# Attention and squared-ReLU kernel: every engine's instructions in written order, q and k transposed into PSUM banks of their own, and the first loads spread over three queues

## The chip, the cores and the metric

The kernel runs on one core of a Trainium2 chip. The metric is the device time of one execution in microseconds (us). The time before is the median of three runs.

## The reference

Two parts follow each other. The first is causal attention for 8 batch rows ("rows" from here on), 8 heads, 576 positions and a head size of 64. Heads 0 to 3 see the last 32 positions (sliding), heads 4 to 7 every fourth of the last 128 (dilated). The second is a feed-forward layer on the 4608 tokens that come out of it: `relu(x @ w_in)`, squared, times `w_out`. Everything comes and goes as float32.

```python
rel = pos[:, None] - pos[None, :]
mask_plain = (rel >= 0) & (rel < 32)
mask_dil = (rel >= 0) & (rel < 128) & (rel % 4 == 0)
attn = softmax(where(mask, q @ k.T / 8, -1e9))        # per row and head, 576 x 576
x = (attn @ v) as (4608 tokens, 512)
g = maximum(x @ w_in, 0) ** 2                         # w_in 512 x 2048
out = g @ w_out                                       # w_out 2048 x 512
```

## The kernel before

Work is cut in two ways. Attention goes by row `b` (576 tokens). The feed-forward layer goes by chunk `c` of 512 tokens, so there are 9 chunks; chunk `c` needs the attention of rows up to `c`. A chunk is 64 matmuls of 128 x 512 into `ph` tiles (`w_in`, called mm1 here; after every 4 a `ph` is done, ScalarE writes `rt` = relu, VectorE writes `g` = `rt`*`rt`) and 64 into `po` tiles (`w_out`, mm2; after every 16 ScalarE copies `po` to `ot` and SyncE's queue stores it).

Attention of a row has stages:

- Loads. `load_sliding_qk` puts q and k of the sliding heads in `sq`, `load_v` puts v in `sv` (sliding) and `sd` (dilated), all on SyncE's queue (SP). `load_dilated_qk` puts q and k of the dilated heads in `nd` on GpSimd's queue (POOL), which casts to float16 on the way. The two weights come on POOL's queue too.
- Casts. POOL turns `sq` into `nq`, `sv` into `vp` and `sd` into `vd`. Only row 0's `nq` is cast by ScalarE (q) and VectorE (k).
- Transposes. `t_sliding` (tile `pt`) and `t_dilated` (tile `pd`) transpose 12 blocks each on TensorE, k and q in the two banks of one tile; VectorE copies k and ScalarE copies q to `QKTp` and `QKTd`.
- Scores (`ps`, `pz`): ScalarE takes exp into `AT`, VectorE multiplies by the mask.
- Values (`pav`, `paw`): VectorE divides by the sums into `x`. TensorE transposes `x` (`px`, `py`) and VectorE copies it to `xT`, the input of mm1.

`attn(b)` is written between pieces of an earlier chunk: `moe_gen` is a generator that yields after every two matmuls, and `pump(n)` runs n such pieces. A chunk has 64 pieces. Row 1 is written beside the rest of chunk 0 and row `b` beside chunk `b-1`; chunks 7 and 8 come alone at the end.

What is written is not what runs: a scheduler takes the instructions and places them on each engine by its own estimate of when they are ready. It may move a load of row 1 ahead of a cast of row 0. Each engine then runs its list strictly in that order; on SP, an issue that waits holds back every issue behind it.

PSUM has two pools: `papool` with 2 tiles of two banks (all attention tiles) and `pmool` with 4 of one bank (`ph`, `po`). The pool `osb` has 3 `ot` tiles, so the copy of the fourth `po` of a chunk waits until the first `ot` is stored.

The parts that the change touches:

Of the kernel before, what the change touches and what calls it, by code (L numbers as in the profile page):

```python
# [17 lines left out]
def kernel(  # L18
# [32 lines left out]
    PADD = P - QD  # L51
    UW = 576
# [16 lines left out]
    QKTd = const.tile([P, 2, HH, 2, PADD + CL], FP16, name="QKTd")  # L69
# [11 lines left out]
    def load_sliding_qk(b):  # L81
        for i, src in enumerate((q, k)):
            nc.sync.dma_start(
                out=sq[:, i, :, :],
                in_=src[b, 0:HH].rearrange("h (p j) d -> p h (j d)", j=6),
            )

    def load_v(b):
        for m in range(NB):
            lo = QB * m - PADP  # L90
            p0 = PADP if m == 0 else 0
            nc.sync.dma_start(  # L92
                out=sv[p0:P, m, :, :],
                in_=v[b, 0:HH, lo + p0 : lo + P, :].transpose([1, 0, 2]),
            )
        vv = v[b, HH:H].rearrange("h (i c) d -> i h (c d)", c=DIL)
        nc.sync.dma_start(out=sd[PADD:P, 0, :, :], in_=vv[0:QD])
        nc.sync.dma_start(out=sd[:, 1, :, :], in_=vv[QD - PADD : CL])

    def load_dilated_qk(b):  # L100
        nd = natp.tile([QB, 2, 2, 12 * D], FP16, name=f"nd{b}", tag="nd")
        for i, src in enumerate((q, k)):
# [3 lines left out]
        return nd  # L106
# [24 lines left out]
    def cast_sliding_qk(b, engs):  # L131
        n = natp.tile([QB, 2, 6, HH, D], FP16, name=f"nq{b}", tag="nq")
        for i in range(2):
            for half in range(2):
                j0 = 3 * half
                copy(
                    engs[i],
# [5 lines left out]
    def cast_v_sliding():  # L143
# [3 lines left out]
    def cast_v_dilated():  # L147
# [17 lines left out]
    make_identity(nc, ident)  # L165
    reli = const.tile([P, QB], I16, name="reli")
    nc.gpsimd.iota(reli, pattern=[[1, QB]], base=0, channel_multiplier=-1)
# [17 lines left out]
    nc.vector.memset(QKTd[:, 1, :, :, 0:PADD], 0.0)  # L185
# [14 lines left out]
    def moe_gen(c):  # L200
        g = gp.tile([P, NFF, TOKC], FP16, name=f"g{c}", tag="g")
        for ffc in range(NFF):
            ph = pmool.tile([P, TOKC], FP32, name=f"ph{c}_{ffc}", tag="pm")
            for dmk in range(NDM):
# [3 lines left out]
                    xT[:, dmk, c * TOKC : (c + 1) * TOKC],  # L208
# [8 lines left out]
            yield  # L217
        for t in range(TOKC // P):
            po = pmool.tile([P, DM], FP32, name=f"po{c}_{t}", tag="pm")
            for ffc in range(NFF):  # L220
                nc.tensor.matmul(  # L221
                    po,
                    g[:, ffc, t * P : (t + 1) * P],
                    wo[:, ffc, :],
                    start=(ffc == 0),
                    stop=(ffc == NFF - 1),
                )
                if ffc % 2 == 1 and ffc < NFF - 1:
                    yield
            ot = osb.tile([P, DM], FP32, name=f"ot{c}_{t}", tag="ot")  # L230
            nc.scalar.copy(ot, po)  # L231
            nc.sync.dma_start(
                out=out[(c * 4 + t) * P : (c * 4 + t + 1) * P, :], in_=ot
            )
            yield

# [15 lines left out]
    def t_sliding(b, n, hp):  # L252
        pt = pa(f"pt{b}_{hp}", FP16)
        for i in (1, 0):
            for j in range(6):
                nc.tensor.transpose(  # L256
                    pt[:, i, QB * j : QB * (j + 1)],
                    n[:, i, j, 2 * hp : 2 * hp + 2, :],
                    ident[0:QB, 0:QB],
                )  # L260
        for i, eng in ((1, nc.vector), (0, nc.scalar)):
            copy(
                eng,
                QKTp[:, i, hp, PADP:].rearrange("x (p j) -> x p j", j=6),
                pt[:, i, 0:UW].rearrange("x (j p) -> x p j", j=6),
            )

    def t_dilated(b, n, g):
        pt = pa(f"pd{b}_{g}", FP16)
        for i in (1, 0):  # L270
            for j in range(6):
                nc.tensor.transpose(  # L272
                    pt[:, i, QB * j : QB * (j + 1)],
                    n[:, i, g, P * j : P * (j + 1)],
                    ident[0:QB, 0:QB],
                )
        for i, eng in ((1, nc.vector), (0, nc.scalar)):
            for h in range(2):
                copy(
                    eng,  # L280
                    QKTd[:, i, 2 * g + h, :, PADD:].rearrange("x a (p s) -> x a p s", s=3),
                    pt[:, i, 0:UW].rearrange("x (s a h p) -> x a h p s", a=2, h=2, p=48)[
                        :, :, h
                    ],
                )
# [22 lines left out]
    def s_dilated(b, g):  # L308
        tiles = [pa(f"pz{b}_{g}_{h}") for h in range(2)]
        for h, ps in enumerate(tiles):  # L310
            for a in range(2):
                for t in range(2):
                    for e in range(2):
# [4 lines left out]
                            QKTd[r, 1, 2 * g + h, a, QD * t : QD * t + P],  # L318
                            QKTd[r, 0, 2 * g + h, a, PADD + QD * t : PADD + QD * (t + 1)],
# [48 lines left out]
    def x_sliding(b, half, xs):  # L368
        px = pa(f"px{b}_{half}", FP16)
        for m3 in range(3):  # L370
            m = 3 * half + m3
            x = xs[m // 2][:, m % 2].rearrange("p h d -> p (h d)")
            for c in range(2):
                nc.tensor.transpose(
                    px[:, 0, 288 * c + QB * m3 : 288 * c + QB * (m3 + 1)],
# [4 lines left out]
        nc.vector.tensor_copy(  # L380
            xT[:, 0:2, t0 : t0 + 288],
            px[:, 0, 0:UW].rearrange("x (c t) -> x c t", c=2),
        )

    def x_dilated(b, t, xs):
        py = pa(f"py{b}_{t}", FP16)
# [117 lines left out]
```

## Time and profile before

| What | Value |
|---|---|
| Time, median of 3 runs | 355.31 us (355.0 to 355.32) |
| The profiled execution | 355.09 us, of which 353.3 us are the span of its instructions |
| TensorE matmul busy | 318.3 us (90%) |
| VectorE, ScalarE, GpSimd busy | 192.2 us (54%), 158.9 us (45%), 83.2 us (24%) |
| DMA | 40.81 MB by the bytes that the packets wrote, mean 116 GB/s |
| Chain that ended last | PE 61%, DMA 16%, ACT 7%, DVE 6% |

In the rows of the profile PE is TensorE, PEld its weight loads, DVE VectorE, ACT ScalarE, POOL GpSimd; SPq and POOLq are the queues' issues. `[6.85 <-DMA nd]` behind an instruction says that its engine had been idle for 6.85 us and what ended that. A matmul's busy time overlaps that of its neighbours, so the distance between two starts is the better measure of what a matmul costs.

### The profile page before, as it was taken

The numbers are of one execution on the slowest core, as the hardware profiler recorded it, in microseconds if no ns is written. First come the engines' busy times: TensorE is split into PE (matmuls) and PEld (weight loads), VectorE is DVE, ScalarE is ACT, GpSimd is POOL, SyncE is SP. The second block draws the span as 40 slices with busy tenths as digits, with TensorE's granted clock in tenths as the row PEclk, the third lists the DMA queues.
The fourth block names the chain that finished last, engine by engine and source line by source line (L and its number), as shares of the span: only waits on it lengthen the run. The fifth ranks groups of instructions, "written<-read, shape, count | busy, mean of one in ns | idle before, by whom it ended". The sixth has DMA issues, their size and how long they took to land.

```text
span 353.3 us, 6704 instructions
## 1 busy us (share of the span) xinstructions
PE 318.3 (90%) x2656; PEld 164.3 (46%) x2656; DVE 192.2 (54%) x422; ACT 158.9 (45%) x296; POOL 83.2 (24%) x130
## 2 busy tenths in 40 slices
PE   0468875996999999999999999999999999999995
PEld 0355332553455545554555455545554554444442
DVE  2676951764874576557655775577557653402400
ACT  3250641605931594149414941494149415614611
POOL 3471527057252322232223222002200000000000
PEclk9999996999999999999999999999999999999999
DMA  8999999959994482448243424300110011011011
GB/s 183 224 211 202 208 254 194 207 131 258 248 196 129 141 170 58 129 128 188 58 125 118 67 58 129 115 2 3 61 60 0 2 68 52 0 61 59 1 61 60
DMA packets 49840, 40.81 MB, mean 116 GB/s; under 512 B 26000, under 2 KB 44688, under 8 KB 49808
## 3 DMA queue, kind: packets, MB, share of 16 engines
q1 hardware_dynamic: 42528, 31.46, 35.1%
q0 software_dynamic: 7280, 8.92, 15.0%
q8 instruction: 21, 0.34, 0.4%
q14 instruction: 11, 0.09, 0.1%
HBM read 39.85 MB, written 9.44 MB: 139 GB/s over the span
## 4 chain that ended last, share of the span: by engine, by line
PE 61%; DMA 16%; ACT 7%; DVE 6%; issue 4%; POOL 2%; SPq 2%; POOLq 0%; ACTq 0%
PE po L221 31%; PE ph L205 22%; DMA sq<-in_k_dram 5%; DMA wi<-in_moe_w_in_dram 4%; DMA sq<-in_q_dram 3%; ACT rt L215 3%; DVE QKTd L129 3%; DVE g L216 2%; DMA sv<-in_v_dram 2%; SPq L92 2%; PE paw L359 2%; DMA out_dram<-ot 2%; ACT QKTd L127 1%; PE pt L256 1%; POOL nq L129 1%
## 5 line engine op out<-in xcount | busy, mean ns | idle before, releaser
L205 PE MATMUL ph<-xT,wi 128*128 128x512 f16 x576 | 139.1, 382 | 2.3 <-ACT rt L215 1.0
L221 PE MATMUL po<-wo,g 128*128 128x512 f16 x576 | 140.1, 381 | 0.0
L215 ACT ACTIVATE rt<-ph 128x512 f16<-128x512 f32 x144 | 84.9, 608 | 36.2 <-PE ph L205 32.8
L216 DVE TENSOR_TENSOR g<-rt 128x512 f16<-128x512 f16 x144 | 68.7, 480 | 58.5 <-ACT rt L215 56.0
L205 PEld LDWEIGHTS <-wi 128*128 128x128 f16 x576 | 51.6, 98 | 57.5 <-issue 3.7
L231 ACT COPY ot<-po 128x512 f32<-128x512 f32 x36 | 21.1, 586 | 121.4 <-PE po L221 110.7
L221 PEld LDWEIGHTS <-g 128*128 128x128 f16 x576 | 51.4, 98 | 50.2 <-issue 0.6
L129 POOL CAST nq<-sq 96x768 f16<-96x768 f32 x28 | 24.1, 894 | 43.3 <-PE pt L256 20.7
L145 POOL CAST vp<-sv 128x512 f16<-128x512 f32 x24 | 16.3, 682 | 74.3 <-PE pav L345 35.3
L150 POOL CAST vd<-sd 128x512 f16<-128x512 f32 x32 | 19.5, 624 | 32.9 <-PE paw L359 25.6
L288 ACT ACTIVATE AT<-ps 128x576 f16<-128x576 f32 x32 | 19.8, 671 | 11.2 <-PE ps L298 11.2
L331 DVE TENSOR_TENSOR x_d<-paw,rcp_d 72x512 f16<-72x512 f32 x32 | 22.0, 686 | 1.1
L272 PE MATMUL pd<-ident,nd 96*128 96x96 f16 x192 | 12.1, 219 | 10.2 <-DMA nd<-in_k_dram 6.8
L256 PE MATMUL pt<-ident,nq 96*128 96x96 f16 x192 | 11.7, 215 | 10.1 <-DVE nq L129 9.6
L129 DVE COPY QKTp<-pt 128x576 f16<-128x576 f16 x16 | 12.0, 756 | 14.1 <-PE pt L256 14.1
L288 ACT ACTIVATE AT<-pz 128x576 f16<-128x576 f32 x32 | 19.1, 650 | 0.1
L289 DVE TENSOR_TENSOR AT<-AT,maskp 128x576 f16<-128x576 f16 x32 | 15.0, 468 | 7.5 <-ACT AT L288 5.1
L129 DVE COPY QKTd<-pd 128x288 f16<-128x288 f16 x32 | 13.0, 448 | 9.2 <-PE pd L272 9.1
L272 PEld LDWEIGHTS <-nd 96*128 96x128 f16 x192 | 11.1, 105 | 14.0 <-issue 10.9
L398 DVE COPY xT<-py 128x576 f16<-128x576 f16 x16 | 12.1, 757 | 9.9 <-PE py L392 9.9
L256 PEld LDWEIGHTS <-nq 96*128 96x128 f16 x192 | 10.6, 103 | 13.6 <-DVE nq L129 9.6
L289 DVE TENSOR_TENSOR AT<-AT,maskd 128x576 f16<-128x576 f16 x32 | 15.1, 474 | 3.2 <-ACT AT L288 0.3
(51 smaller groups left out, 194.5 us busy)
## 6 DMA issues: line engine op xcount, KB each, us to landing
out_dram<-ot SPq DMA_DIRECT2D x36, 256.0 KB, 2.4
sv<-in_v_dram SPq DMA_DIRECT2D x40, 128.0 KB, 4.4
sq<-in_q_dram SPq DMA_DIRECT2D x8, 576.0 KB, 10.5
sq<-in_k_dram SPq DMA_DIRECT2D x8, 576.0 KB
sd<-in_v_dram SPq DMA_DIRECT2D x8, 512.0 KB
nd<-in_q_dram POOLq DMA_DIRECT2D x16, 144.0 KB, 5.8
nd<-in_k_dram POOLq DMA_DIRECT2D x16, 144.0 KB, 6.0
sd<-in_v_dram SPq DMA_DIRECT2D x8, 288.0 KB
```

The costliest lines, as they stand in the source:

```text
L129: eng.tensor_copy(o, i)
L150: nc.gpsimd.tensor_copy(vd[:, t, c : c + 2, :, 0:D], sd[:, t, :, D * c : D * (c + 2)].rearrange("p h (c d) -> p c h d", d=D),)
L205: nc.tensor.matmul(ph, wi[:, dmk, ffc * P : ffc * P + P], xT[:, dmk, c * TOKC : (c + 1) * TOKC], start=(dmk == 0), stop=(dmk == NDM - 1),)
L215: nc.scalar.activation(rt, ph[:], ACTF.Relu)
L216: nc.vector.tensor_mul(g[:, ffc, :], rt, rt)
L221: nc.tensor.matmul(po, g[:, ffc, t * P : (t + 1) * P], wo[:, ffc, :], start=(ffc == 0), stop=(ffc == NFF - 1),)
L231: nc.scalar.copy(ot, po)
L256: nc.tensor.transpose(pt[:, i, QB * j : QB * (j + 1)], n[:, i, j, 2 * hp : 2 * hp + 2, :], ident[0:QB, 0:QB],)
L272: nc.tensor.transpose(pt[:, i, QB * j : QB * (j + 1)], n[:, i, g, P * j : P * (j + 1)], ident[0:QB, 0:QB],)
L288: nc.scalar.activation(AT[:, u, 0:UW], ps[:, :, 0 : UW // 2], ACTF.Exp, scale=scale)
L289: nc.vector.tensor_mul(AT[:, u, 0:UW], AT[:, u, 0:UW], mask)
L331: nc.vector.tensor_tensor(out=x[0:w], in0=pv[:, :, :, 0:D], in1=rcp[0:w].unsqueeze(3).to_broadcast([w, 2, HH, D]), op=ALU.mult,)
```

## The change

The scheduler is switched off (`manual_schedule`): each engine gets its instructions in the order of the program text, and the text is rearranged. With it come these edits.

1. Row 0's loads. k of the sliding heads and both dilated v loads are issued from ScalarE's queue; q and sliding v stay on SP. POOL makes `reli` and the identity first, and loads dilated k before q. The cast of k is shared by VectorE and POOL, that of q stays on ScalarE.
2. q and k are transposed into a bank each (`pt`, `pd` are now one-bank tiles, four times two per row), from `pmool`, or from `papool` in row 1, where `po` holds all four banks of `pmool`. `QKTd` has another layout. `px` and `py` come from `pmool` too, and ScalarE instead of VectorE copies them to `xT`.
3. Row 0 alternates transposes and scores. Row 1's loads come after three `ph` of chunk 0; row 1's q and k go before `w_out`, its v after its sliding transposes.
4. Chunk 0's mm2 runs over four `po` at once, four rows of `w_out` at a time (`mm2_by_rows_gen`), so that it can start when a quarter of `w_out` is there. All four outputs are then done at the end.
5. From row 2 on: transposes with 2 pieces of mm1 after each half, scores with 4 after each, values with 2 (1 in row 2).

```diff
+    ctx.enter_context(tc.manual_schedule())
...
-    load_sliding_qk(0)
-    nds = {0: load_dilated_qk(0)}
-    load_v(0)
+    load_sliding_qk(0, (nc.sync, nc.scalar))
+    reli = const.tile([P, QB], I16, name="reli")
+    nc.gpsimd.iota(reli, pattern=[[1, QB]], base=0, channel_multiplier=-1)
+    make_identity(nc, ident)
+    nds = {0: dilated_buffer(0)}
+    load_dilated_qk(0, nds[0])
+    load_sliding_v(0)
+    load_dilated_v(0, nc.scalar)
...
+    def mm2_by_rows_gen(c, g):
+        pos = [
+            pmool.tile([P, DM], FP32, name=f"po{c}_{t}", tag="pm") for t in range(TOKC // P)
+        ]
+        for f4 in range(0, NFF, 4):
+            for t, po in enumerate(pos):
+                for ffc in range(f4, f4 + 4):
+                    mm2(c, g, po, t, ffc)
+                    if ffc % 2 == 1 and ffc < NFF - 1:
+                        yield
+                if f4 + 4 == NFF:
+                    store(c, t, po)
+                    yield
...
+    def pt(name, wide):
+        if wide:
+            return pa(name, FP16)[:, 0, :]
+        return pmool.tile([P, 1024], FP16, name=name, tag="pm")
+
+    def t_sliding(b, n, hp, i, wide=False):
+        p_ = pt(f"pt{b}_{hp}_{i}", wide)
+        for j in range(6):
+            nc.tensor.transpose(
+                p_[:, QB * j : QB * (j + 1)],
+                n[:, i, j, 2 * hp : 2 * hp + 2, :],
+                ident[0:QB, 0:QB],
+            )
+        copy(
+            nc.vector if i else nc.scalar,
+            QKTp[:, i, hp, PADP:].rearrange("x (p j) -> x p j", j=6),
+            p_[:, 0:UW].rearrange("x (j p) -> x p j", j=6),
+        )
...
-    def attn(b, nq, nd, gap):
...
+    nq = cast_sliding_qk(0, (nc.scalar, nc.scalar, nc.vector, nc.gpsimd))
+    cast_sliding_v()
+    load_w_in()
+    cast_dilated_v()
+    for hp in range(2):
+        for i in (1, 0):
+            t_sliding(0, nq, hp, i)
+        s_sliding(0, hp)
...
+    g0 = hidden(0)
+    pending.append(mm1_gen(0, g0))
+    pump(6)
+    nds[1] = dilated_buffer(1)
+    nc.vector.memset(sq[:, :, :, 0:1], 0.0)
+    nc.vector.memset(nds[1][:, :, :, 0:1], 0.0)
+    load_sliding_qk(1)
+    load_dilated_qk(1, nds[1])
+    load_w_out()
+    nq = cast_sliding_qk(1, (nc.gpsimd,) * 4)
+    pump(26)
+    pending.append(mm2_by_rows_gen(0, g0))
+    for hp in range(2):
+        for i in (1, 0):
+            t_sliding(1, nq, hp, i, True)
+            pump(1)
+    nc.vector.memset(sv[:, 1, :, 0:1], 0.0)
+    nc.vector.memset(sd[:, 1, :, 0:1], 0.0)
+    load_v(1)
+    cast_v()
+    load_sliding_qk(2)
+    load_v(2)
+    nds[2] = dilated_buffer(2)
+    load_dilated_qk(2, nds[2])
...
+    attn_scores(1, 3)
+    attn_values(1, 1, True)
+    pump(1000)
...
+        transposes(b, nq, nds[b], 2)
+        attn_scores(b, 4)
+        attn_values(b, 1 if b == 2 else 2)
+        pump(1000)
```

What the order of the instructions shows at three places. First SP's queue before, from row 2's v (`sv`, `sd`) to the first stores of chunk 0 (`ot_0`, `ot_1`); the two `sq` rows after `sd` are row 3's, the third is row 4's q:

```order
L92 DMA sv<-in_v_dram 96x4x64
L92 DMA sv<-in_v_dram 128x4x64 x5
L97 DMA sd<-in_v_dram 72x4x256
L98 DMA sd<-in_v_dram 128x4x256
L83 DMA sq<-in_q_dram 96x4x384
L83 DMA sq<-in_k_dram 96x4x384
L83 DMA sq<-in_q_dram 96x4x384
L232 DMA out_dram<-ot_0_720 128x512
L92 DMA sv<-in_v_dram 96x4x64
L232 DMA out_dram<-ot_1_810 128x512
```

The same place on SP after the change, from row 2's `sq` on:

```order
L90 DMA sq<-in_q_dram 96x4x384
L90 DMA sq<-in_k_dram 96x4x384
L99 DMA sv<-in_v_dram 96x4x64
L99 DMA sv<-in_v_dram 128x4x64 x5
L106 DMA sd<-in_v_dram 72x4x256
L107 DMA sd<-in_v_dram 128x4x256
L251 DMA out_dram<-ot_0_882 128x512
L251 DMA out_dram<-ot_1_915 128x512
L251 DMA out_dram<-ot_2_945 128x512
L251 DMA out_dram<-ot_3_962 128x512
```

Row 3's q and k no longer stand ahead of the first store; all of row 2's loads still do, and all four stores now stand together.

Second ScalarE's list before, where chunk 0 ends and chunk 1 begins (`pz` are row 1's last scores, `pt` row 2's transposes):

```order
L288 ACTIVATE AT<-pz_1_1_755 128x576
L231 COPY ot_1_810<-po_1_723 128x512
L231 COPY ot_2_921<-po_2_821 128x512
L231 COPY ot_3_951<-po_3_934 128x512
L215 ACTIVATE rt_0_1002<-ph_0_955 128x512
L127 COPY QKTp<-pt_0_985 128x576
L215 ACTIVATE rt_1_1010<-ph_1_1005 128x512
L127 COPY QKTp<-pt_1_1013 128x576
```

The same place after the change:

```order
L431 COPY xT<-px_1_872 128x2x288
L250 COPY ot_0_882<-po_0_586 128x512
L250 COPY ot_1_915<-po_1_587 128x512
L449 COPY xT<-py_0_933 128x2x288
L250 COPY ot_2_945<-po_2_588 128x512
L449 COPY xT<-py_1_948 128x2x288
L250 COPY ot_3_962<-po_3_589 128x512
L235 ACTIVATE rt_0_971<-ph_0_966 128x512
L235 ACTIVATE rt_1_979<-ph_1_974 128x512
L235 ACTIVATE rt_2_987<-ph_2_982 128x512
L235 ACTIVATE rt_3_995<-ph_3_990 128x512
L235 ACTIVATE rt_4_1003<-ph_4_998 128x512
```

The copy to `ot_3`, which reuses `ot_0`'s tile, stands ahead of every `rt` of chunk 1 in both; the four `ot` copies have moved together to the end of row 1, and row 2's transposes have moved behind six `ph`.

Third POOL's list before, from row 0's v casts to row 1's q and k:

```order
L145 CAST vp<-sv 128x8x64 x3
L110 DMA wi<-in_moe_w_in_dram 128x4x512 x2
L110 DMA wi<-in_moe_w_in_dram 128x4x1024
L150 CAST vd<-sd 128x8x64 x4
L117 DMA wo<-in_moe_w_out_dram 128x4x512 x4
L105 DMA nd_502<-in_q_dram 48x2x768 x2
L105 DMA nd_502<-in_k_dram 48x2x768 x2
L129 CAST nq_579<-sq 96x768 x4
```

And after the change:

```order
L143 CAST nq_141<-sq 96x768
L159 CAST vp<-sv 128x8x64 x3
L124 DMA wi<-in_moe_w_in_dram 128x4x512 x2
L124 DMA wi<-in_moe_w_in_dram 128x4x1024
L164 CAST vd<-sd 128x8x64 x4
L120 DMA nd_456<-in_k_dram 48x2x768 x2
L120 DMA nd_456<-in_q_dram 48x2x768 x2
L131 DMA wo<-in_moe_w_out_dram 128x4x512 x4
L143 CAST nq_469<-sq 96x768 x4
```

`w_in` still stands right behind the casts of row 0's sliding v; row 1's dilated q and k have moved ahead of `w_out`.

More of the change, by code (lines that the diff above doesn't have):

```diff
@@ L51 @@
     PADD = P - QD
+    KPAD = 64
     UW = 576
@@ L217, in moe_gen, with mm2, store, mm2_gen @@
             yield
+    def mm2(c, g, po, t, ffc):
+        nc.tensor.matmul(
+            po,
+            g[:, ffc, t * P : (t + 1) * P],
+            wo[:, ffc, :],
+            start=(ffc == 0),
+            stop=(ffc == NFF - 1),
+        )
+    def store(c, t, po):
+        ot = osb.tile([P, DM], FP32, name=f"ot{c}_{t}", tag="ot")
+        nc.scalar.copy(ot, po)
+        nc.sync.dma_start(out=out[(c * 4 + t) * P : (c * 4 + t + 1) * P, :], in_=ot)
+    def mm2_gen(c, g):
         for t in range(TOKC // P):
@@ L220, in moe_gen, with hidden @@
             for ffc in range(NFF):
[L221 to L227, printed above, removed]
+                mm2(c, g, po, t, ffc)
                 if ffc % 2 == 1 and ffc < NFF - 1:
                     yield
[L230 to L234, printed above, removed]
-            yield
+            store(c, t, po)
+            yield
+    def mm2_by_rows_gen(c, g):
[5 more added lines that the diff above has]
+                for ffc in range(f4, f4 + 4):
+                    mm2(c, g, po, t, ffc)
+                    if ffc % 2 == 1 and ffc < NFF - 1:
+                        yield
+                if f4 + 4 == NFF:
+                    store(c, t, po)
+                    yield
+    def hidden(c):
+        return gp.tile([P, NFF, TOKC], FP16, name=f"g{c}", tag="g")
+    def moe_gen(c):
+        g = hidden(c)
+        yield from mm1_gen(c, g)
+        yield from mm2_gen(c, g)
     pending: list = []
@@ L423, in attn @@
             pump(gap)
[L424 to L431 removed]
+        x_sliding(b, 0, xs, wide)
+        pump(gap)
+        ys = [av_dilated(b, 0, 0)]
+        pump(gap)
+        x_sliding(b, 1, xs, wide)
+        pump(gap)
+        ys.append(av_dilated(b, 0, 1))
         pump(gap)
```

197 lines of the change are left out of this document (88 added, 109 removed).

## The prediction

> **What bounds the kernel now.** I read the slices of the page first, then the windows of the trace by row of attention, then the chain that ended last, then the engines' timelines around its waits.
>
> ```profile
> span 353.3 us, 6704 instructions
> PE   0468875996999999999999999999999999999995
> PEclk9999996999999999999999999999999999999999
> DMA  8999999959994482448243424300110011011011
> ```
>
> A slice is 8.83 us. TensorE is full from about the tenth slice on; before that it is not, and there DMA is. The kernel has a front of some 80 us that DMA paces and a steady part of 270 us that TensorE paces. The windows (PE, PEld, DVE, ACT, POOL busy, clock, DMA share, GB/s) put numbers to both:
>
> ```profile
> 0.00:70.00 70.00, 44.60 (x423) 25.37 (x423) 39.93 (x89) 27.43 (x50) 28.39 (x48) 0.95 1.12 210
> 55.00:60.00 5.00, 2.69 (x22) 1.47 (x23) 0.82 (x2) 0.33 (x1) 4.87 (x8) 0.50 1.17 172
> 116.34:151.99 35.65, 34.96 (x317) 18.30 (x316) 22.18 (x48) 17.79 (x34) 10.18 (x15) 1.00 0.52 127
> ...
> 187.64:223.30 35.66, 34.97 (x317) 18.30 (x316) 22.19 (x48) 17.79 (x34) 10.19 (x15) 1.00 0.38 93
> 223.30:258.50 35.20, 34.99 (x318) 18.31 (x317) 21.66 (x48) 17.79 (x34) 4.46 (x7) 1.00 0.09 35
> 258.50:293.70 35.20, 34.99 (x318) 18.31 (x317) 21.57 (x48) 17.79 (x34) 0.00 (x0) 1.00 0.08 31
> 293.70:321.30 27.60, 27.60 (x130) 12.48 (x129) 6.80 (x16) 11.90 (x20) 0.00 (x0) 1.00 0.10 39
> ```
>
> In 70 us the rings never empty: 210 GB/s. Rows 3, 4 and 5 take 35.65 us each, rows 6 and 7 35.20. The last line is a chunk without attention: 128 matmuls in 27.60 us, 0.2156 us each. So a row's attention costs TensorE 35.20 - 27.60 = 7.6 us where POOL is idle.
>
> Where front and steady part meet, the chain shows what ends the wait, and TensorE's and ScalarE's timelines agree:
>
> ```profile
> 76.52 5.51 DMA out_dram<-ot
> 82.13 0.59 ACT ot L231
> ...
> 116.94 0.51 PE pt L256 x12
> ```
>
> ```profile
> 49.65 0.81 PE L221 MATMUL po<-wo,g 128*128 128x512 f16 x3
> 57.31 1.12 PE L272 MATMUL pd<-ident,nd 96*128 96x96 f16 x12 [6.85 <-DMA nd<-in_k_dram]
> 82.77 0.59 PE L205 MATMUL ph<-xT,wi 128*128 128x512 f16 x2 [0.95 <-ACT ot L231]
> ```
>
> There are two stops. At 50.5 us TensorE waits 6.85 us for row 1's dilated k. At 82 us ScalarE waits for the first store of chunk 0 to land, because the fourth `ot` copy needs its tile; every `rt` of chunk 1 stands behind that copy, and TensorE has run out of `pmool` banks after three `ph` (12 matmuls) and 24 transposes of row 2. The copy ends at 82.13 + 0.59 = 82.72.
>
> **The change, part by part.** The stop at 57.3 should go, since row 1's q and k now go ahead of `w_out`, with only row 0 and `w_in` ahead of them. How early is that?
>
> ```profile
> 35.81 8.91 DVE L216 TENSOR_TENSOR g<-rt 128x512 f16<-128x512 f16 x11 [1.31 <-ACT rt L215]
> 36.61 3.13 POOL L129 CAST nq<-sq 96x768 f16<-96x768 f32 x4
> ```
>
> Before, chunk 0's first `g` is at 35.81, so its third, after which the loads are issued now, is at about 37.5. If row 0's attention gets shorter (copies that no longer wait for each other, k cast on two engines, against more waiting in written order) it comes sooner; I bound it by 32.5 and 37.5. Then 1,152 KB of `sq` and 576 KB of `nd` are 8.2 us at 210 GB/s, their landing 2 and four casts 3.1. Row 1's transposes can run at 46 to 51 us instead of 57.3. With the same spacing as before from there, chunk 1 starts 7 us sooner, at about 71.2: before it was 78.2 (82.77 less 0.95 idle, 2.6 for 12 matmuls and 1.0 for 24 transposes). Three `ph` later, at about 73.7, TensorE is at the second stop. That stop stays: ScalarE's list still has the `ot_3` copy ahead of all `rt`, and on SP the first store stands behind all of row 2's loads. Between 71 and 81 it makes no difference when TensorE gets there.
>
> So I price the moment at which the first store lands. These are the issues and what each moves (KB; us from issue to landing last):
>
> ```profile
> out_dram<-ot SPq DMA_DIRECT2D x36, 256.0 KB, 2.4
> sv<-in_v_dram SPq DMA_DIRECT2D x40, 128.0 KB, 4.4
> sq<-in_q_dram SPq DMA_DIRECT2D x8, 576.0 KB, 10.5
> sd<-in_v_dram SPq DMA_DIRECT2D x8, 512.0 KB
> nd<-in_q_dram POOLq DMA_DIRECT2D x16, 144.0 KB, 5.8
> sd<-in_v_dram SPq DMA_DIRECT2D x8, 288.0 KB
> wo<-in_moe_w_out_dram POOLq DMA_DIRECT2D x4, 512.0 KB, 23.3
> wi<-in_moe_w_in_dram POOLq DMA_DIRECT2D x2, 512.0 KB, 12.6
> wi<-in_moe_w_in_dram POOLq DMA_DIRECT2D x1, 1024.0 KB, 18.6
> sv<-in_v_dram SPq DMA_DIRECT2D x8, 96.0 KB, 9.0
> ```
>
> A row (k like q) is 1,152 + 736 + 800 + 576 = 3,264 KB, the weights 4,096 KB. Ahead of the first store stand three rows and both weights: 13,888 KB. Row 0 alone is 15.5 us at 210 GB/s, so it is in at about 17 us.
>
> ```profile
> 15.15 0.62 POOL L145 CAST vp<-sv 128x512 f16<-128x512 f32 x1 [0.98 <-DMA sv<-in_v_dram]
> 15.71 2.26 POOL L110 DMA_DIRECT2D wi<-in_moe_w_in_dram  x3
> ```
>
> `w_in` is issued behind the last `vp` cast, and before, row 1's loads filled the time until its data flowed. Now those loads wait for chunk 0, so the rings run dry. A POOL issue of 144 KB lands after 5.8 us, of which 0.7 are transfer; with 1.2 us for the landing of `sv` (a 256 KB store lands after 2.4, of which 1.2 are transfer) and 0.6 for the cast the gap is about 6.8 us. The gap's bounds are 0 (another queue still busy) and the 12.6 of `w_in`'s own issue to landing. So `w_in` flows from 23.8 us and 10,624 KB remain. At 210 GB/s they take 50.6 us, at 172, the slowest row above, 61.8. I take 195 (54.5 us), nearer the first, since it moves the same transfers, but lower, since the weights now run alone for longer. Then 23.8 + 54.5 + 2.4 + 0.6 = 81.3 us for the end of the `ot_3` copy, against 82.72: **1.4 us earlier**, with ends at 77.4 and 88.6.
>
> At that point less is done than before: the 24 transposes of row 2 come later now. They cost twice 0.51: **+1.0 us**. And TensorE has then idled from 73.7 to 81.3. Before, after 6.85 us of idling, the granted clock is 0.50 for the window at 55 us and full again in the slices after; TensorE worked at half rate for 3.4 us of it at most: **+1.7 us** lost. Ends: 0 if the idle time is shorter, 3.4 if it is half rate twice as long.
>
> For the steady rows these are the costs. TensorE's waits inside a row (two matmuls of `ph` are 0.43 us):
>
> ```profile
> 229.49 0.60 PE L205 MATMUL ph<-xT,wi 128*128 128x512 f16 x2
> 230.16 0.30 PE L298 MATMUL ps<-QKTp 64*128 64x96 f16 x6
> ...
> 233.41 0.60 PE L205 MATMUL ph<-xT,wi 128*128 128x512 f16 x2
> 234.16 0.30 PE L298 MATMUL ps<-QKTp 64*128 64x96 f16 x6
> ```
>
> 229.49 + 0.43 leaves 0.24 us before 230.16, and 233.41 + 0.43 leaves 0.32 before 234.16. Both end with ScalarE, whose copies wait for VectorE's copy of the other bank:
>
> ```profile
> 227.05 0.64 ACT L127 COPY QKTp<-pt 128x576 f16<-128x576 f16 x1 [0.54 <-DVE QKTp L129]
> 230.49 1.21 ACT L288 ACTIVATE AT<-ps 128x576 f16<-128x576 f32 x2
> 235.55 1.13 ACT L215 ACTIVATE rt<-ph 128x512 f16<-128x512 f32 x2
> ```
>
> With a bank each that wait goes, and all transposes stand ahead of all scores. The row then is 27.60 + 7.6 - 0.56 = 34.64 us. Two things eat into it. In the scores each group now comes with two `ph`: ScalarE needs 1.21 + 1.13 = 2.34 us for it and TensorE four matmul pairs (1.72) and about 0.5, 2.2 us. ScalarE falls back 0.1 us per group; the banks hold that, and I put 0.1 us on the row (ends 0 and 0.5). And VectorE shares something with POOL:
>
> ```profile
> L216 DVE TENSOR_TENSOR g<-rt x16: 412/426/3818, 35.8 to 48.6; 128x512 f16<-128x512 f16 x16
> 119.33 3.52 POOL L129 CAST nq<-sq 96x768 f16<-96x768 f32 x4 [6.92 <-PE pt L256]
> ```
>
> One `g` of chunk 0, all of them between 35.8 and 48.6, took 3.82 us instead of 0.43 while POOL cast `nq`. The rows with POOL at work cost 35.65 against 35.20, 0.45 more; with later scores I take 0.25 for a row with casts. So rows 3 to 5 come to 35.0 us (3 x 0.65 gained), row 6 to 35.0 (0.2), row 7 to 34.75 (0.45): **2.6 us gained**, ends 0 and 4. Row 2 runs from the resume: 116 matmuls (25.0) + 7.04 + 0.35 = 32.4 us. Before it took 116.34 - 82.72 = 33.6 with 1.0 of transposes already done, 34.6 in the same terms: **2.2 us gained**.
>
> ScalarE's four new `xT` copies fall in mm2, where it is idle most of the time, and chunks 7 and 8 don't change: nothing for both. Without that idle time each copy would cost ScalarE about what a `QKTp` copy does, 0.64 us.
>
> Sum: -1.4 + 1.0 + 1.7 - 2.6 - 2.2 = -3.5 us on the profiled execution's own 355.09 us (its span and 1.8 us around it), which is 0.2 below the median: **351.6 us**.
>
> **The rivals.** (a) The first store lands before TensorE needs it. Then TensorE never idles: it resumes at 73.7 instead of 81.3 and the 1.7 us of half clock go, so 351.6 - 7.6 - 1.7 = 342.3 us. For it: 7 us of the front's gain are real. Against: 13.9 MB ahead of that store need 66 us even at 210 GB/s, and to land by 73 they would have to flow at 215 or more from the start, without any gap.
>
> (b) Slower: the rings run worse once SP and POOL no longer feed them side by side all the time. At the 172 GB/s of one window above the stream takes 61.8 us, the copy ends at 88.6 and the time is 351.6 + 7.3 = 358.9. It decides from a rate of 180 GB/s down, where the copy ends at 85.8 and the gains in the steady rows are used up (355.9). For it: `w_out` has some 10 us alone. Against: 210 on average over 70 us with every mix of transfers in it.
>
> (c) POOL holds VectorE for its whole burst of casts, as at 36 us, in every steady row with casts, because the four `nq` casts now fall between `g`s that ScalarE's three `rt` tiles wait for. A block of 3.5 us against 2.6 us of slack (three `rt`, 0.86 each) costs 0.9 us instead of 0.25 in rows 2 to 6: 351.6 + 5 x 0.65 = 354.9. Against: at 119.33 in steady rows the same burst made a row only 0.45 longer. [...]
>
> **How the numbers follow.** My forecast, copy ending between 79 and 84.5, has 0.53 and gives 349 to 355; (a) and what lies toward it 0.15; (b) 0.20; (c) 0.12. A difference of 0.2% (0.7 us) is about what a measurement of this kernel can tell. Faster: 0.53 + 0.15 and a third of (c), 0.72; same: the rest of (c), 0.08; slower: 0.20. The range goes from 344, most of the way to (a), to 357, the middle of (b); the forecast's own is 349 to 355.
>
> **What would show it.** The chain should pass through a store of `ot` into the `ot` copy shortly after 81 us, with a stop of some 8 us on TensorE ahead of it, 12 matmuls into chunk 1, and a clock row of 0.5 there. Rows 3 to 7 should be 34.7 to 35.1 us apart. ScalarE's `QKTp` copies should no longer wait for VectorE. No stop near 57 us on `nd`. If TensorE's longest stop is not at that store, or it ends before 77, the forecast is wrong toward (a); if DMA shows gaps or under 180 GB/s between 24 and 78 us, toward (b).

## The result, and the profile after

The changed kernel takes 347.06 us (median of 3 runs, 346.15 to 347.51) against 355.31: a ratio of 0.977 (95% interval 0.973 to 0.980), 8.25 us faster. The forecast was 351.6. Of two of the later kernels one run each, the profiled one, took about 2% or more longer than their other runs at a lower granted clock (377.57 us for the written order alone, 356.23 us for `xT` on VectorE), and it is left out of the times and ratios given for them. The profiled execution of the changed kernel has a span of 345.7 us, 7.6 less than before. The page's slices:

```profile
span 345.7 us, 6713 instructions
PE   0669979937999999999999999999999999999995
PEclk9999999996999999999999999999999999999999
DMA  8894999997923990579058905890110010011011
```

A slice is now 8.64 us. The dip of TensorE near 57 us is gone. A deep one stands in the ninth and tenth slices, with a lowered clock in the tenth. Here is the stop on TensorE, then on ScalarE, then the issues on SP ahead of it (start, busy, and in brackets the idle time before):

```profile
69.32 2.75 PE L225 MATMUL ph<-xT,wi 128*128 128x512 f16 x12
79.55 4.85 PE L225 MATMUL ph<-xT,wi 128*128 128x512 f16 x12 [7.47 <-ACT ot L250]
...
78.92 0.58 ACT L250 COPY ot<-po 128x512 f32<-128x512 f32 x1 [9.42 <-DMA out_dram<-ot]
...
57.70 0.47 SPq L90 DMA_DIRECT2D sq<-in_k_dram  x1
58.27 10.41 SPq L99 DMA_DIRECT2D sv<-in_v_dram  x6
68.77 0.97 SPq L106 DMA_DIRECT2D sd<-in_v_dram  x1
69.83 1.23 SPq L107 DMA_DIRECT2D sd<-in_v_dram  x1
71.16 8.70 SPq L251 DMA_DIRECT2D out_dram<-ot  x4
```

Chunk 1 starts at 69.32. TensorE does 12 matmuls in 2.75 us, idles 7.47 us until the `ot_3` copy is through, and then needs 4.85 us for 12 matmuls like the first 12, so 2.1 us go to the clock (0.50 granted from 77.01 to 83.84 us). The store that the copy waits for is issued at 71.16, behind the last load of row 2. This is the stop that the prediction described. The windows by row (PE, PEld, DVE, ACT, POOL busy, clock, DMA share, GB/s):

```profile
69.32:113.86 44.54, 37.06 (x318) 18.64 (x317) 20.02 (x44) 20.67 (x39) 18.87 (x30) 0.92 0.73 154
113.86:148.44 34.58, 34.56 (x317) 18.16 (x316) 20.91 (x44) 20.35 (x38) 10.26 (x15) 1.00 0.61 141
148.44:182.86 34.42, 34.42 (x318) 18.23 (x317) 20.57 (x44) 20.45 (x38) 10.42 (x15) 1.00 0.60 127
...
251.86:286.27 34.41, 34.41 (x317) 18.22 (x316) 19.15 (x44) 20.45 (x38) 0.00 (x0) 1.00 0.09 32
286.27:313.90 27.63, 27.63 (x130) 12.55 (x129) 6.80 (x16) 11.89 (x20) 0.00 (x0) 1.00 0.10 39
```

A row that took 35.65 us takes 34.4 to 34.6, and whether POOL casts in it (10.42) or not (0.00) makes no difference. Row 2 takes 44.54, with the stop in it. Last, what the DMA rings did in the front:

```profile
16.50:19.50 3.00, 1.92 (x28) 1.44 (x28) 1.92 (x4) 1.92 (x5) 3.00 (x6) 1.00 0.23 17
19.50:29.50 10.00, 7.22 (x102) 5.77 (x103) 7.78 (x19) 3.39 (x6) 2.31 (x4) 1.00 1.17 207
29.50:35.50 6.00, 6.00 (x22) 2.32 (x21) 1.73 (x6) 2.92 (x6) 0.51 (x1) 1.00 0.01 3
35.50:78.50 43.00, 34.21 (x308) 16.78 (x306) 18.34 (x43) 18.42 (x33) 20.64 (x33) 0.98 1.12 223
```

There are two holes: 3 us ahead of `w_in`, and 6 us behind it, in which 3 GB/s flow, because row 1's loads wait for the third `g` of chunk 0 (it starts at 34.23, they are issued from 34.75 on). After that 223 GB/s flow for 43 us.

By TensorE's end (349.07 before, 341.69 after) the terms of the prediction's sum measure as follows. Row 2 is 113.86 - 79.50 = 34.36 us from the resume; less the 2.1 at half clock that is 32.26, against 33.62 + 1.0 before. Rows 3 to 7 are 286.27 - 113.86 against 293.65 - 116.34.

| Term | Forecast, us | Measured, us |
|---|---|---|
| End of the `ot_3` copy (82.72 before) | -1.4 | -3.2 (79.50) |
| 24 transposes of row 2 later | +1.0 | +1.0 (taken over) |
| Half clock behind the stop | +1.7 | +2.1 |
| Row 2 from the resume | -2.2 | -2.4 |
| Rows 3 to 7 | -2.6 | -4.9 |
| Sum | -3.5 | -7.4 |

So two things were to be settled: what the stop at the store hangs on and costs, and why the rows gained nearly twice what was forecast.

### The profile page after: what moved, and what is told of

Same layout as the page of the kernel before. It is cut to its first block, busy times and chain, and to the rows that moved or that the text cites. A ratio compares the mean times of both kernels' runs of the same rounds, so it can differ in the third digit from the quotient of the medians.

```text
span 345.7 us, 6713 instructions
## 1 busy us (share of the span) xinstructions
PE 316.1 (91%) x2656; PEld 163.5 (47%) x2656; DVE 173.2 (50%) x390; ACT 181.0 (52%) x328; POOL 83.9 (24%) x131
## 4 chain that ended last, share of the span: by engine, by line
PE 79%; DMA 12%; DVE 3%; ACT 2%; POOL 1%; issue 1%; SPq 0%; ACTq 0%; POOLq 0%; DVEq 0%
PE ph L225 34%; PE po L240 32%; DMA sq<-in_k_dram 8%; PE pt L309 2%; DMA out_dram<-ot 2%; PE paw L410 2%; PE pd L323 2%; DMA sv<-in_v_dram 2%; PE pav L396 2%; PE ps L348 2%; PE pz L367 1%; POOL nq L143 1%; PE px L425 1%; ACT AT L338 1%; PE py L443 1%; DVE AT L339 1%
## 5 line engine op out<-in xcount | busy, mean ns | idle before, releaser
L225 PE MATMUL ph<-xT,wi 128*128 128x512 f16 x576 | 141.5, 387 | 7.5 <-ACT ot L250 7.5
L236 DVE TENSOR_TENSOR g<-rt 128x512 f16<-128x512 f16 x144 | 66.2, 465 | 80.3 <-ACT rt L235 79.2
L143 POOL CAST nq<-sq 96x768 f16<-96x768 f32 x29 | 25.7, 924 | 72.0 <-DMA sq<-in_k_dram 72.0
L431 ACT COPY xT<-px 128x576 f16<-128x576 f16 x16 | 10.2, 638 | 32.6 <-PE px L425 32.6
L309 PE MATMUL pt<-ident,nq 96*128 96x96 f16 x192 | 14.4, 215 | 11.1 <-DVE nq L143 9.3
L339 DVE TENSOR_TENSOR AT<-AT,maskp 128x576 f16<-128x576 f16 x32 | 19.0, 617 | 6.0 <-ACT AT L338 5.3
L309 PEld LDWEIGHTS <-nq 96*128 96x128 f16 x192 | 12.1, 103 | 18.4 <-DVE nq L143 9.3
L449 ACT COPY xT<-py 128x576 f16<-128x576 f16 x16 | 10.2, 639 | 13.9 <-PE py L443 13.8
L382 DVE TENSOR_TENSOR x_p<-pav,rcp_p 96x512 f16<-96x512 f32 x24 | 16.5, 687 | 0.8
L410 PEld LDWEIGHTS <-AT 128*128 128x128 f16 x256 | 12.6, 102 | 8.4 <-PE paw L410 1.7
## 6 DMA issues: line engine op xcount, KB each, us to landing
out_dram<-ot SPq DMA_DIRECT2D x36, 256.0 KB, 2.1
```

The source lines that it names most:

```text
L143: eng.tensor_copy(o, i)
L225: nc.tensor.matmul(ph, wi[:, dmk, ffc * P : ffc * P + P], xs[:, dmk, :], start=(dmk == 0), stop=(dmk == NDM - 1),)
L236: nc.vector.tensor_mul(g[:, ffc, :], rt, rt)
L309: nc.tensor.transpose(p_[:, QB * j : QB * (j + 1)], n[:, i, j, 2 * hp : 2 * hp + 2, :], ident[0:QB, 0:QB],)
L339: nc.vector.tensor_mul(AT[:, u, 0:UW], AT[:, u, 0:UW], mask)
L382: nc.vector.tensor_tensor(out=x[0:w], in0=pv[:, :, :, 0:D], in1=rcp[0:w].unsqueeze(3).to_broadcast([w, 2, HH, D]), op=ALU.mult,)
```

## The experiments: the front

**Four `ot` tiles.** The stop's direct cause taken away:

```diff
+    otp = ctx.enter_context(tc.tile_pool(name="otp", bufs=4))
-        ot = osb.tile([P, DM], FP32, name=f"ot{c}_{t}", tag="ot")
+        ot = otp.tile([P, DM], FP32, name=f"ot{c}_{t}", tag="ot")
```

> The changed kernel with four `ot` tiles instead of three, so the copy of `ot_3` of chunk 0 waits for no store. Theory (that one wait is the whole of the stop before 80 us): TensorE's idle 7.47 us and the 2.15 us that it loses at half clock behind it both go; 347.06 - 9.6 = 337.4 us, chunk 1 runs through from about 69.3, no clock row of 0.5 after 60 us. Rival (row 2's data are the next wait: its casts and `nd` are in at 72.1 and 74.8 in the changed kernel, its `vd` casts at 79.5): a new stop at the row 2 transposes or values takes at least 3 us of it back, 340.5 or more.

Measured: 338.22 us, ratio 0.953 (0.949 to 0.958). Its windows for rows 2 and 3:

```profile
70.66:105.46 34.80, 34.80 (x318) 18.13 (x316) 21.60 (x44) 20.98 (x39) 16.58 (x26) 1.00 0.86 187
105.46:139.87 34.41, 34.41 (x317) 18.24 (x316) 20.46 (x44) 20.48 (x38) 10.51 (x15) 1.00 0.64 140
```

Row 2 is 34.80 us instead of 44.54, with a full clock. The stop with what followed from it cost 9.7 us in row 2; chunk 1 starts 1.3 us later here (70.66), so the whole gains 8.8. TensorE waits for no data of row 2, and the rival falls.

**Chunk 0's stores on ScalarE's queue.** Three `ot` tiles, but the stores no longer stand behind row 2's loads:

```diff
-        nc.sync.dma_start(out=out[(c * 4 + t) * P : (c * 4 + t + 1) * P, :], in_=ot)
+        (nc.scalar if c == 0 else nc.sync).dma_start(out=out[(c * 4 + t) * P : (c * 4 + t + 1) * P, :], in_=ot)
```

> The changed kernel with chunk 0's four stores issued from ScalarE's queue instead of SP's; three `ot` tiles as before. Theory (what holds the first store is its place on SP behind row 2's loads): it is issued right behind its copy at 65.8 and lands before 72 us even when it shares the rings; the stop is 1 us or less, no half clock; 338 to 339 us. Rival (the rings are simply full until 79 us, whatever queue the store is on): it lands near 77, 345 to 347 us.

Measured: 343.05 us, ratio 0.967 (0.964 to 0.971), between the two. ScalarE's list:

```profile
67.62 0.38 ACTq L251 DMA_DIRECT2D out_dram<-ot  x1
...
74.77 0.59 ACT L250 COPY ot<-po 128x512 f32<-128x512 f32 x1 [3.04 <-DMA out_dram<-ot]
76.09 0.34 ACTq L251 DMA_DIRECT2D out_dram<-ot  x1
```

The store is issued at 67.62 instead of 71.16 but lands only just ahead of 74.77, 7.1 us later. So its place on SP is worth about 4 us (78.92 to 74.77). The rest is time to landing: chunk 0's four stores take 6.1 to 7.9 us from issue to landing here, where the median store of the changed kernel lands after 2.1 us. That the loads which share the rings with them make the difference is an inference. TensorE's stops in chunk 1 shrink to 1.3, 0.8 and 0.8 us. Neither theory's number was right.

**Row 1's loads before chunk 0.** This fills the 6 us hole:

```diff
-    pump(6)
     nds[1] = dilated_buffer(1)
     ...
-    pump(26)
+    pump(32)
```

> The changed kernel with row 1's loads (and the two memsets that hold them back) written ahead of chunk 0's first `ph` instead of behind the third; three `ot` tiles. It fills the 6 us in which the rings are empty (29.6 to 35.7). Theory (the DMA stream as a whole sets the landing of the first store): loads issued near 28.5, the store lands 4 to 6 us sooner, the stop shrinks to 2 to 4 us; 341 to 343 us. Rival (SP is held at 50.1 by the `sv` memset behind row 1's transposes, which stand behind mm1 of chunk 0 until 44.8): only the 2.1 us of small stops at 45.8 to 48 move, the store lands some 2 us sooner; 344.5 to 345.5 us.

Measured: 341.69 us, ratio 0.962 (0.958 to 0.965), as the theory has it. Its windows:

```profile
29.50:35.50 6.00, 6.00 (x25) 2.48 (x24) 2.03 (x5) 3.25 (x7) 4.59 (x7) 1.00 1.04 222
35.50:72.80 37.30, 32.91 (x304) 16.39 (x303) 19.09 (x42) 17.91 (x32) 16.92 (x25) 0.99 1.13 222
```

And in its timelines the `ot_3` copy on ScalarE and TensorE's resume:

```profile
73.29 0.58 ACT L250 COPY ot<-po 128x512 f32<-128x512 f32 x1 [6.98 <-DMA out_dram<-ot]
...
73.93 5.26 PE L225 MATMUL ph<-xT,wi 128*128 128x512 f16 x12 [5.04 <-ACT ot L250]
```

Where 3 GB/s flowed there are 222 now, and the copy starts at 73.29 instead of 78.92: 5.6 us sooner for 6 us of hole filled. The stream as a whole sets the landing of the first store. The rival's gate on SP did not hold it. The time gains 5.4 us.

**Both.**

> Four `ot` tiles and row 1's loads ahead of chunk 0's first `ph`. Theory (with the stop at the store gone TensorE sets the end, and the loads are worth the small stops at 45.8 to 48 alone): 337.4 - 2.1 = 335.3 us. Rival (row 1's loads share the rings with `w_in` and make chunk 0 later): 337.5 or more.

Measured: 334.94 us, ratio 0.944 (0.941 to 0.946): faster than both kernels by a clear margin, and within 0.4 of the theory. Its page:

```profile
PE   0569999999999999999999999999999999999995
PEclk9999999999999999999999999999999999999999
```

From the fourth slice to the last but one TensorE is full, and no slice from there on shows a lowered clock.

**Row 0's loads from SP again**, in this fastest version:

```diff
-    load_sliding_qk(0, (nc.sync, nc.scalar))
+    load_sliding_qk(0)
-    load_dilated_v(0, nc.scalar)
+    load_dilated_v(0, nc.sync)
```

> The fastest version so far (four `ot` tiles, row 1's loads early, 334.9 us) with k and dilated v of row 0 issued from SP again. Theory (row 0 waits for its bytes: 16 us of full rings whichever queue issues them, and mm1 of chunk 0 starts when row 0's attention is through): chunk 0 starts within 1 us of 29.05, 334.5 to 336 us. Rival (SP's issues come late, one every 0.5 us and only eight in flight, so dilated v lands later and `w_in` with it): chunk 0 starts 1.5 us later or more, 336.5 us or more.

Measured: 336.3 us, ratio 0.947 (0.941 to 0.954), an interval that holds the 0.944 of the version with ScalarE's queue. In the traces chunk 0 starts at 29.39 instead of 29.05, and chunk 1 at 68.12 instead of 68.08. The time lies between the theory's range and the rival's; the start of chunk 0 is the theory's. Issuing from ScalarE is worth nothing that this measures.

## The experiments: the rows

**The banks undone, the order kept.** In rows 2 to 7 one two-bank tile holds k and q again:

```diff
         for hp in range(2):
-            for i in (1, 0):
-                t_sliding(b, nq, hp, i, wide)
-                pump(gap)
+            p2 = pa(f"pt{b}_{hp}", FP16)      # 6 + 6 transposes into its two banks,
+            ...                               # then both copies (t_dilated likewise)
+            pump(2 * gap)
```

> The changed kernel with the banks alone undone, in rows 2 to 7: k and q of a pair of heads are transposed into the two banks of one `papool` tile again, 12 transposes in a row, then both copies, then the same number of pieces of mm1. Order and front stay. Theory B (the prediction's: the 0.56 us per row came from two copies waiting for each other): rows 3 to 7 go from 34.4 to 35.0 us, 347.06 + 6 x 0.56 = 350.4 us. Rival O (the order did it: with all transposes ahead of all scores no score waits for a copy that was made just before it): rows stay within 0.1 of 34.4, 346.5 to 347.7 us, and ScalarE's copies wait for VectorE's again at no cost.

Measured: 363.13 us, ratio 1.020 (1.014 to 1.026): slower than the kernel before. TensorE's timeline in row 6:

```profile
237.95 0.30 PE L350 MATMUL ps<-QKTp 64*128 64x96 f16 x6
240.28 0.30 PE L350 MATMUL ps<-QKTp 64*128 64x96 f16 x6 [2.03 <-ACT QKTd L141]
```

and row 5 as a window:

```profile
192.16:228.46 36.30, 34.73 (x317) 18.26 (x316) 20.13 (x44) 19.71 (x38) 9.84 (x15) 1.00 0.56 121
```

The scores wait some 2 us per row for ScalarE's `QKTd` copies. They don't read `QKTd`: the second of their two tiles is the `papool` tile that these copies still empty. In the program each first ScalarE copy of a shared tile waits for VectorE's semaphore; with a bank each it waits for TensorE's alone (rows 3 to 7). Rows 3 to 7 average 36.85 us (chunk 7 starts at 301.37, chunk 2 at 117.14). Rival O falls: the written order alone doesn't do it, it makes the shared tile worse. Theory B has the cause, but its 0.56 per row was far too little for this order.

**The banks alone**, in the kernel before with its scheduler:

```diff
-        pt = pa(f"pt{b}_{hp}", FP16)
+        pts = [pmool.tile([P, 1024], FP16, name=f"pt{b}_{hp}_{i}", tag="pm") for i in range(2)]
         ...                                   # pt[:, i, x] becomes pts[i][:, x]; t_dilated likewise
```

> The kernel before, with its scheduler and text, and only the banks changed: q and k of `pt` and `pd` in one-bank tiles of `pmool`. Theory B: the waits of 0.24 and 0.32 us go, rows of 35.65 become about 35.1 and rows of 35.18 about 34.6, 355.3 - 3.4 = 352 us. Rival O: rows stay within 0.15 of the kernel before; 355.3, or above it by what the transposes lose by sharing four banks with `ph` and `po`.

Measured: 347.49 us, ratio 0.976 (0.971 to 0.981). That is the whole net gain of the change. Its windows for rows 3, 4 and 7:

```profile
113.94:148.34 34.40, 34.40 (x318) 18.22 (x316) 22.55 (x48) 18.12 (x34) 10.17 (x15) 1.00 0.52 133
148.34:182.74 34.40, 34.40 (x318) 18.21 (x317) 22.54 (x48) 18.12 (x34) 10.18 (x15) 1.00 0.52 125
251.53:285.92 34.39, 34.39 (x317) 18.23 (x316) 21.71 (x48) 18.11 (x34) 0.00 (x0) 1.00 0.09 32
```

Its longest stop on TensorE, in the front, is still the one on `nd`:

```profile
56.30 1.12 PE L276 MATMUL pd<-ident,nd 96*128 96x96 f16 x12 [7.53 <-DMA nd<-in_k_dram]
```

With the old text, the scheduler and `xT` copied by VectorE, rows are 34.40 us, with casts and without. The order is not quite the old one: where the scheduler split the scores of a pair of heads into two groups with two `ph` between, it now leaves them in one. So the 0.8 to 1.25 us that a row gains are the banks' effect and that of the order which the scheduler makes of them. Row 3 starts at 113.94, in the changed kernel at 113.86: the new front had gained by 69.32 and given it back at the store.

**The written order alone**: `manual_schedule` in the kernel before, nothing else.

> The kernel before with the scheduler switched off and nothing else: its own text, in written order. Theory O in its strong form (following the text is worth it by itself): rows under 35 us. Theory B: rows stay at 35.2 to 35.7, because banks and text are as before. For the front both expect a loss: row 1's loads are then issued behind all of `w_out` and behind 15 pieces of chunk 0, 5 us or more, so 356 to 365 us in all.

Measured: 369.9 us, ratio 1.038 (1.030 to 1.045). A row in its trace, which is of the run of 377.57 us:

```profile
159.82:199.89 40.07, 36.48 (x317) 18.90 (x316) 23.28 (x48) 17.88 (x34) 10.27 (x15) 0.96 0.51 110
```

Rows take 37 to 41 us there; the granted clock of this one is 0.96 on average. If all 7.7 us between that run and 369.9 lay in rows 3 to 7, these would still average 37.9 us, by this estimate. The strong form of O falls. Theory B expected 35.2 to 35.7 and is wrong in size. In this trace the scores wait for `QKTd` copies as in the kernel with the banks undone, 17.6 us in ten waits from 120 us on, so the scheduler had been hiding most of the shared tile's price. The old text in written order with a bank each was not run.

**The changed text, scheduled.** `manual_schedule` taken out of the changed kernel.

> The changed kernel's text, with its banks, given to the scheduler again. Theory O: the scheduler moves transposes, scores and pieces as before, rows of 34.4 go to 35 or more, 350 us or more. Theory B: with the banks kept the rows stay at 34.4 to 34.6, and what changes is the front alone (the scheduler may issue loads at another place), 343 to 351 us.

Measured: 355.8 us, ratio 1.001 (0.998 to 1.003). Rows 3 to 7 are 34.41 to 34.42 us, as B says, so the rest is the front: the scheduler puts the last `xT` copy of row 1 behind the `ot_3` copy on ScalarE.

```profile
84.59 0.58 ACT L249 COPY ot<-po 128x512 f32<-128x512 f32 x1 [15.24 <-DMA out_dram<-ot]
85.07 0.65 ACT L448 COPY xT<-py 128x576 f16<-128x576 f16 x1
...
85.77 6.79 PE L224 MATMUL ph<-xT,wi 128*128 128x512 f16 x20 [15.32 <-ACT xT L448]
```

TensorE does four matmuls of chunk 1 and then idles 15.32 us, twice what it does in written order. The time came out above the range that B gave.

**Own banks, taken from `papool`:**

```diff
-        wide = gap == 0
+        wide = True
-                t_dilated(b, nd, g, i, wide and not i)
+                t_dilated(b, nd, g, i, wide)
```

> The changed kernel with a bank each for k and q still, but in rows 2 to 7 that bank is taken from the two tiles of `papool`, where the scores and values live, instead of from `pmool`. It parts two things that the shared two-bank tile did at once: ScalarE's copy waits for VectorE's, and the tile keeps scores out of `papool`. Theory S (the copies in series are the cost): rows 2 to 7 stay at 34.4 to 34.6, 347 us. Theory P (the held tile is the cost, since the first scores wait until both copies of the last transposes are done): a stop at the first `ps` of each row, rows of 35 or more, over 350 us. With the two mixed, between.

Measured: 347.68 us, ratio 0.978 (0.972 to 0.984); rows 3 to 7 of 34.41 us and no wait on TensorE in them. So holding a tile of `papool` costs nothing by itself; it costs where the copies are in series and ScalarE's, the later one, keeps the tile. Copies in series from a tile outside `papool` were not tried.

**POOL's casts doubled** in rows 3 to 7:

```diff
         nq = cast_sliding_qk(b, (nc.gpsimd,) * 4)
+        if b > 2:
+            again(b, nq)                      # the same four casts once more
         cast_v()
+        if b > 2:
+            cast_v()
```

> The changed kernel with every POOL cast of rows 3 to 7 done twice in a row (the same values written again), so POOL is busy some 20 us a row instead of 10. Rival (c) of the prediction, and its charge of 0.25 us per row for POOL and VectorE: five rows get 0.25 to 0.9 us longer each, 348.3 to 351.5 us. Theory (VectorE loses time to POOL, 1.4 us a row already, but nothing that TensorE waits for): rows stay at 34.4, 347 us; VectorE's busy time in a row grows by another 1 to 1.5 us.

Measured: 360.28 us, ratio 1.014 (1.009 to 1.020), far above what rival (c) gave and against the theory. The timelines of VectorE and of POOL in row 4:

```profile
164.07 1.97 DVE L348 TENSOR_TENSOR AT<-AT,maskp 128x576 f16<-128x576 f16 x2
165.97 2.00 DVE L245 TENSOR_TENSOR g<-rt 128x512 f16<-128x512 f16 x2
167.89 2.07 DVE L348 TENSOR_TENSOR AT<-AT,maskp 128x576 f16<-128x576 f16 x2
...
164.69 2.04 POOL L143 CAST nq<-sq 96x768 f16<-96x768 f32 x2
166.68 3.96 POOL L161 CAST nq<-sq 96x768 f16<-96x768 f32 x4
```

Row 5 as a window:

```profile
189.85:226.75 36.90, 34.74 (x318) 18.09 (x317) 23.39 (x44) 20.47 (x38) 18.14 (x26) 1.00 0.54 120
```

From 164 to 170 us each mask and nearly each `g` takes about 1.0 us, the length of one cast, instead of 0.4 to 0.5. The changed kernel has this too, for four casts:

```profile
157.12 3.74 POOL L143 CAST nq<-sq 96x768 f16<-96x768 f32 x4 [12.57 <-DMA sq<-in_k_dram]
...
159.11 2.07 DVE L339 TENSOR_TENSOR AT<-AT,maskp 128x576 f16<-128x576 f16 x2
161.10 0.74 DVE L236 TENSOR_TENSOR g<-rt 128x512 f16<-128x512 f16 x2
161.77 0.81 DVE L339 TENSOR_TENSOR AT<-AT,maskp 128x576 f16<-128x576 f16 x2
```

There VectorE has made up its delay before the values, and TensorE waits for nothing. With eight casts it has not: four `pav` of rows 3 to 6 wait 7.9 us in all for VectorE. So (c) did not come as it was written: no operation is held for a whole burst, the longest `g` of these rows takes 1.04 us, with the casts single or doubled, and the longest mask of the changed kernel 1.07. While POOL casts, these operations of 0.4 to 0.5 us take up to about one cast's length each, 1.0 us. The single burst costs TensorE nothing, the doubled casts 2.5 us in row 5. The doubled casts of v are a part of this run, too, and were not tried apart. What the two engines share, no run shows.

**`xT` copied by VectorE again:** `nc.scalar.copy` becomes `nc.vector.tensor_copy` at both places.

> The changed kernel with the four `xT` copies of a row on VectorE again. Theory (off the path on either engine, as the prediction's zero says): 347 us, rows of 34.4. Rival (VectorE, slowed by POOL, is then late for the masks or the `g` behind a copy of 0.64 us or more): rows of 34.6 or more in rows 2 to 6, 348 us or more.

Measured: 348.34 us, ratio 0.980 (0.974 to 0.986), which overlaps that of the changed kernel (0.973 to 0.980): no difference shown, though the time lies in the rival's range. The trace, of the run of 356.23 us, has a granted clock of 0.945 (0.95 from 150 to 200 us), so its rows can't be compared; in it TensorE waits for nothing in rows 3 to 7. With the banks alone VectorE copies `xT` too, and the rows are 34.40 us.

## Why the prediction was right or wrong

**The stop at the first store: right, and early by 1.8 us.** The chain goes through the store, the stop comes 12 matmuls into chunk 1 and lasts 7.47 us (some 8 forecast), the clock is lowered behind it. The number behind it, 81.3, was put together from a hole and a rate that were both off. One hole of 6.8 us was priced where there are 3 us, and a second of 6 us, behind `w_in`, was not seen, although the prediction itself had row 1's loads wait for chunk 0's third `g`. The rate was taken at 195 GB/s against 207 and 223. The units slipped as well: a 128x512 float32 tile is listed as 256.0 KB, so a KB is 1,024 bytes, while GB/s count 10^9. 10,624 KB at 195 GB/s are 55.8 us and not 54.5, and the term would have been -0.1 us instead of -1.4. These errors partly cancelled; that the stop came where it was forecast is right by its cause, that 81.3 came so near to 79.50 is in part luck. Rival (b) falls with the rate: the sign named for it, a gap between 24 and 78 us, did show, but nothing near 172 GB/s occurred behind it.

**Rival (a) did not happen, but its price was good.** It gave 9.3 us for the stop and its clock; four `ot` tiles removed 9.7 from row 2.

**Half clock: +2.1 against +1.7**, a small miss of size. Stop at 57 us gone, ScalarE's `QKTp` copies of rows 3 to 7 without a wait for VectorE, `xT` copies free: as forecast.

**The rows: this is the step that failed.** 35.0 us was forecast per row with casts, 34.75 without; they are 34.4 to 34.6, and the term of -2.6 us measured -4.9. That is 2.3 of the 3.9 us by which the sum missed; the end of the copy makes another 1.8. The cause named for the rows, copies of one tile that wait for each other, was right; two sizes in it were wrong.

First, the shared tile was priced at TensorE's two visible gaps, 0.24 and 0.32 us. Both stand in the middle of the scores of a pair of heads: six `ps`, two `ph`, six `ps` (the prediction's rows from 229.49 and 233.41 on). With the banks alone, row 7 has the twelve in one group:

```profile
257.48 0.43 PE L302 MATMUL ps<-QKTp 64*128 64x96 f16 x12
257.84 1.47 PE L205 MATMUL ph<-xT,wi 128*128 128x512 f16 x6
```

By the starts in the traces a change from `ph` to `ps` costs 0.10 us even where nothing waits (0.31 us to the next start instead of 0.216), and the change back 0.115 (0.135 instead of 0.02 on average). So the 0.24 and 0.32 were 0.14 and 0.22 of waiting and a change each, and the two changes back, 0.23 more, were not seen. Together that is 0.79; rows without casts gained 0.77 (35.18 to 34.41; 34.39 with the banks alone). The program text has nothing between the two groups, and in written order with the shared tile TensorE stands still between them; that the scheduler put the `ph` there to cover this wait is inferred. TensorE's busy time hid most of it, 34.99 us before and 34.41 after: a matmul's recorded 0.38 us run past the start of the next, 0.216 us after its own, so a start that comes a little late leaves no idle time. "7.6 us of attention" thus contained waits and changes. Second, the 0.25 kept for POOL and VectorE was no cost of its own. In the kernel before, ScalarE's first `QKTd` copies in row 3, where POOL casts `nq` at that time, and in row 6, where it does not:

```profile
122.93 0.70 ACT L127 COPY QKTd<-pd 128x288 f16<-128x288 f16 x2 [0.73 <-DVE QKTd L129]
...
229.41 0.70 ACT L127 COPY QKTd<-pd 128x288 f16<-128x288 f16 x2 [0.25 <-DVE QKTd L129]
```

The wait for VectorE is 0.48 us longer where POOL casts, about the 0.45 by which such rows were longer. POOL's delay reached TensorE through the two copies in series, so it went with them; the banks alone make both kinds of rows equal. The 0.1 us for ScalarE's scores did not show either.

The shared tile had k and q in different banks and its copies still waited for each other, by a semaphore of VectorE that stands in the program (the 0.73 and 0.25 us above). With a bank each the program has no such wait. So it belonged to how the program guards a tile; what would happen without a guard was not run.

**What the change is made of.** The banks alone give 347.49, everything together 347.06. The written order alone costs some 14 us, and with the shared tile in the rows the changed kernel is at 363. The new front gains nothing net until the store's wait is taken out: then it and the earlier loads bring 12 us more (334.94). Four `ot` tiles with the old front were not run.

## What to carry to other kernels

When two engines empty halves of one tile, look whether the second waits for the first in the trace, and give each half a tile of its own: that made every steady row 0.8 to 1.2 us shorter here, and in the changed kernel's written order the shared tile costs 16 us (363.13 against 347.06). Before a stage is priced at its engine's busy time, compare the starts of its instructions with a place where nothing waits, and count how often it changes from one kind of work to the other (0.10 or 0.115 us a change here). When a front gets faster, follow the first buffer that comes free only by a store: a fourth 256 KB output tile was worth 9 us, because the store stood behind a whole row of loads.

## What the runs showed of the hardware that was not expected

While TensorE has work, the granted clock's records of the two kernels show one stretch of half rate each: 53.87 to 60.70 us in the kernel before, around the stop of 6.85 us, and 77.01 to 83.84 us in the changed kernel, around the one of 7.47. Both are 6.83 us long; TensorE resumed 3.39 us before the end of the first and 4.29 us before the end of the second. Of shorter stops, one of 1.8 us (four `ot` tiles) left the profiled execution at a granted clock of 1.00. With the banks undone, row 4 (153.44 to 192.16 us) has 2.58 us in which TensorE is not busy and a clock of 0.96, row 5 has 1.57 us and 1.00. And a stop of 5.04 us cost no less at the clock (5.26 instead of 2.75 us for 12 matmuls, with row 1's loads early) than one of 7.47 (4.85). What sets the start and the length of a stretch, these runs do not show.

The records begin at 33.39 us in the kernel before and at 32.64 in the changed kernel. A 9 in the clock row or a 1.00 in a window ahead of that is no reading: in the changed kernel the matmuls of chunk 0 from 30.3 to 32.4 us start 0.43 us apart, twice the later 0.216.
